# Values' copy in DRAM: rows by place then chunk, window reads that alternate between the two partition halves

## The chip, the core and the metric

The kernel runs on one core of a Trainium2 chip. A core has a matrix engine (TensorE, here PE, with its weight loads as PEld), three engines for elementwise work (VectorE or DVE, ScalarE or ACT, GpSimd or POOL), SyncE (SP), which only issues transfers, and 16 DMA engines that move all data between DRAM (HBM) and the on-chip memory of 128 partitions. Transfers issued by POOL go through queue q0, those of SP through q1, those of ACT through q10; all three share the 16 DMA engines. The metric is the device time of one execution in microseconds.

## The reference

Chunked attention over 4 batches, 8 heads, 768 tokens, head size 64, followed by a mixture of experts that takes the two best of 8 experts per token. Only the windows matter here.

```python
chunk, left_ctx, right_ctx = (32, 16, 8)
for c in range(nc):                       # 24 chunks of 32 tokens
    l_start = max(0, c * chunk - left_ctx)
    r_end = min(S, c * chunk + chunk + right_ctx)
    k_full = np.concatenate([mem_k, k[:, :, l_start:r_end]], axis=2)
    v_full = np.concatenate([mem_v, v[:, :, l_start:r_end]], axis=2)
    a = softmax(scale * q_c @ k_full.T)
    out[:, :, c_start:c_end] = np.matmul(a, v_full)
# then: x = out as [3072, 512]; logits = x @ w_gate, noisy top 2 of 8,
# out = sum of top2_w * (relu(x @ w1[e]) @ w2[e])
```

Each chunk of 32 queries sees 8 memory rows and a window of 56 rows: 16 before the chunk, the chunk itself, 8 after.

## The kernel before

There are two stages, attention with routing and then the experts. Attention runs over 4 batches of 3 steps, each step t covering 256 tokens. A step has these parts. `scores` (L402 on) multiplies queries by keys and subtracts the row maximum on VectorE. `exps` takes the exponential on ScalarE. `turn_p` transposes the probabilities on PE. `values` (L441 on, products at L453) multiplies them by the values, and VectorE scales the result (L460). `turn_x` and `gate` compute the router's logits. Before the first step of a batch `turn` transposes its queries and keys on PE (L393), and VectorE and ScalarE copy them out (L531 for the first batch, L549 for the others). A finished batch is stored to DRAM as `xd` by `keep_x` (L485, issued by ACT, the last part by SP). The routing lists pick rows of `xd` for the experts, whose products are L714 and L726; their weights are loaded by POOL (L78 to L87).

Values need the 64 rows of a window on the partitions: for one chunk, 8 memory rows and then 56 rows of the sequence, for even heads (par 0) on partitions 0 to 63 and for odd heads (par 1) on 64 to 127. This regrouping goes through DRAM. For each batch b:

- `load_v` (L117) loads the values from f32 to bf16 into `vn`: 128 partitions, six tokens each.
- `spread_v` (L368, two POOL copies) reorders the heads into `vp`, so that a token's row has 256 numbers of the even heads and then 256 of the odd ones.
- `window_v` writes `vp` to the DRAM tile `vd` as rows of 1 KB in the order of the sequence (L374, one transfer issued by SP, 128 runs of 6 KB). Then POOL issues two transfers of the memory rows (L378) and four window reads (L383). A read takes place k of every chunk's window to partition k: for each of 32 (or 24) partitions, 24 runs of 512 B that lie 32 KB apart in `vd`. The first span (r0 = 0) covers places 0 to 31 and the second (r0 = 32) places 32 to 55; the order is par 0 first span, par 0 second span, par 1 first span, par 1 second span.

`vd` has two tiles, for even and odd batches; so have the destination `vb`, the keys and the queries. 16 rows before and 16 after the sequence are filled with zeros once (L156); scores of places outside the sequence are set to a large negative number (L418, L420), so that they get no weight.

The order of all POOL's transfers is pinned as written: v0, k0, q0, then memory rows and window reads of batch 0, v1, q1, k1, the spread of batch 1, v2, memory rows and window reads of batch 1, q2, k2, the spread of batch 2, v3, and so on to the weights of experts 0 to 2. POOL works in order: while it waits for the write of `vd` to land, nothing behind is issued. PE, VectorE, ScalarE and SP follow an order written out by hand (L516 to the end of attention): turns of the next batch's queries and keys stand between the steps of this one.

Semaphores of transfers rotate over eight per kind of queue, so a transfer also waits until the one eight before it has landed.

Of the kernel before, what the change touches and what calls it, by code (L numbers as in the profile page):

```python
# [22 lines left out]
def kernel(  # L23
# [14 lines left out]
    nc = tc.nc  # L38
# [65 lines left out]
    def scratch(n):  # L104
        scol[0] -= n
        return wflat[:, scol[0]:scol[0] + n]
    xrow = [scratch(SO * Dm).rearrange("p (s r) -> p s r", s=SO) for _ in range(2)]
    vn = scratch(H * SO * D).rearrange("p (h c) -> p h c", h=H)
# [5 lines left out]
    vd = [tc.dram_tile([S + CH, Dm], BF16, name=f"vd{i}") for i in range(2)]  # L114

    def load_nat(t, x, b):
        pin(nc.gpsimd.dma_start(out=t, in_=x[b].rearrange("h (p s) d -> p h (s d)", s=SO)))  # L117

    def load_v(b):
        load_nat(vn, v, b)  # L120
# [29 lines left out]
    vp = keep.tile([128, H * SO * D], BF16, name="vp")  # L150
# [3 lines left out]
    for i in range(2):  # L154
        for r0, n in ((0, LC), (LC + S, CH - LC)):
            nc.sync.dma_start(out=vd[i][r0:r0 + n, :], in_=zeros[0:n, :])  # L156


# [4 lines left out]
    for b in range(B):  # L163
        nc.sync.dma_start(out=mvs[b * NM:(b + 1) * NM], in_=mem_v[b].rearrange("h m d -> m h d"))
    mvn = keep.tile([B * NM, Dm], BF16, name="mvn")
# [200 lines left out]
    def spread_v(b):  # L366
        for par in range(2):
            pin(nc.gpsimd.tensor_copy(  # L368
                out=vp.rearrange("p (s a c d) -> p a c s d", s=SO, a=2, c=HP)[:, par],
                in_=vn.rearrange("p (c a) (s d) -> p a c s d", a=2, s=SO)[:, par]))  # L370

    def window_v(b):
        t, o = vb[b % 2], vd[b % 2]
        nc.sync.dma_start(out=o[LC:LC + S, :].rearrange("(p s) c -> p (s c)", s=SO), in_=vp)  # L374
        for par in range(2):
            p0 = par * 64
            cols = slice(par * 256, (par + 1) * 256)
            pin(nc.gpsimd.dma_start(out=t[p0:p0 + NM, par], in_=mvn[b * NM:(b + 1) * NM, cols].unsqueeze(1).to_broadcast([NM, NCH, 256])))  # L378
        for par in range(2):
            p0 = par * 64  # L380
            cols = slice(par * 256, (par + 1) * 256)
            for r0, n in ((0, CH), (CH, WIN - CH)):
                pin(nc.gpsimd.dma_start(out=t[p0 + NM + r0:p0 + NM + r0 + n, par],  # L383
                                        in_=o[r0:r0 + S, cols].rearrange("(c k) w -> k c w", k=CH)[0:n]))
# [601 lines left out]
```

## Time and profile before

| | |
|---|---|
| time, median of 3 runs (lowest, highest) | 360.43 us (359.46, 362.16) |
| the profiled execution: its own time, its span | 358.42 us, 356.7 us |
| PE, DVE, ACT, POOL busy | 80%, 48%, 38%, 38% of the span |
| PE busy in 144 to 350 us (three windows) | 204.3 of 206 us |
| PE busy in 22 to 127 us (five windows) | 72.1 of 105 us |
| mean granted PE clock | 0.867 |
| queue q0 | 34240 packets, 46.82 MB, 73.2% of 16 engines' span |
| write of `vd`, issue to landing | 768 KB x4, median 9.0 us |
| window reads, issue to landing | 384 KB x8, median 13.0 us; 288 KB x8, median 13.3 us |
| POOL's time at an issue of a window read | 745 ns |
| POOL's copies of L368 | 8, 1469 ns each |

The profile is of one execution. A share of busy time is a mean over the span, which here has two stages with different limits; so it is read by stage. The DMA share adds the time of all packets over 16 engines. It goes above 100%, since an engine has more than one packet under way. The trace also holds each packet of a DMA engine with its queue, size, start and duration, called the packet records below; they do not name the engine. Times in the text are microseconds from the start of the span.

### The profile page before, as it was taken

The page shows a single profiled execution, that of the slowest core. Times are in us where ns is not written, and L with a number is a line of the kernel's source. Part 1 is how long each engine was busy: PE and PEld are TensorE (multiplying, and loading weights), DVE is VectorE, ACT ScalarE, POOL GpSimd, SP SyncE. Part 2 cuts the span into 40 slices and gives each one's busy share as a digit, 9 for nine tenths or more (in the row PEclk, how much of TensorE's full clock was granted, in tenths as well). Part 3 has the DMA queues.
Part 4 walks back from the last instruction along what each step waited for, and adds up shares of the span by engine and source line. Part 5 has one row for each costly group of instructions (what it writes and reads, how often), then busy time and mean ns, then how long its engine had stood idle before and what let it go on. Part 6 is the DMA issues. An engine that isn't in the chain of part 4 may idle for free.

```text
span 356.7 us, 7042 instructions
## 1 busy us (share of the span) xinstructions
PE 285.9 (80%) x2934; PEld 186.3 (52%) x2955; DVE 170.3 (48%) x349; ACT 136.9 (38%) x189; POOL 134.3 (38%) x181
## 2 busy tenths in 40 slices
PE   0356577777847732999999999999999999999991
PEld 0245455666736621865544465664455775565540
DVE  7656456699689885531133302954310334223221
ACT  8813645564645610144322343213243222243310
POOL 6460573354453036706530744332580122201122
PEclk9995655565687865699999999999999999999998
DMA  8999999999999999499999999961289971100012
GB/s 122 235 171 169 245 174 208 251 198 211 247 156 208 253 249 180 106 194 143 178 196 235 209 173 252 159 119 51 87 166 189 208 184 54 53 2 2 25 47 81
DMA packets 49866, 56.97 MB, mean 160 GB/s; under 512 B 16931, under 2 KB 39523, under 8 KB 49828
## 3 DMA queue, kind: packets, MB, share of 16 engines
q0 software_dynamic: 34240, 46.82, 73.2%
q1 hardware_dynamic: 13920, 6.62, 10.9%
q10 hardware_dynamic: 1668, 3.02, 2.4%
q8 instruction: 25, 0.41, 0.5%
q14 instruction: 13, 0.11, 0.1%
HBM read 70.39 MB, written 13.96 MB: 236 GB/s over the span
## 4 chain that ended last, share of the span: by engine, by line
PE 33%; issue 20%; POOL 5%; DVE 4%; DMA 3%; POOLq 1%; ACT 0%; DVEq 0%
PE p_h L714 18%; PE p_y L726 13%; POOL out_dram L677 4%; DMA out_dram<-y,main_dst 1%; DMA xTt<-xt 1%; DMA xt<-xd,main_src 1%; POOL xt L671 1%; DVE w_all L460 1%; PE p_xt L691 0%; POOL w_all L844 0%; POOLq L981 0%; DVE mx L423 0%; DVE sc L425 0%; ACT xT L472 0%; PE ps_o L453 0%
## 5 line engine op out<-in xcount | busy, mean ns | idle before, releaser
L714 PE MATMUL p_h<-xTt,w_all 128*128 128x256 bf16 (+3 forms) x669 | 102.7, 313 | 0.7 <-DVE xTt L692 0.5
L726 PE MATMUL p_y<-w_all,h 128*128 128x512 bf16 x446 | 102.3, 379 | 0.9
L714 PEld LDWEIGHTS <-w_all 128*128 128x128 bf16 x736 | 70.0, 101 | 36.3 <-issue 0.7
L702 ACT ACTIVATE h<-p_h 128x512 bf16<-128x512 f32 (+1 forms) x81 | 44.7, 551 | 95.9 <-PE p_h L714 88.3
L726 PEld LDWEIGHTS <-h 128*128 128x128 bf16 x464 | 45.3, 98 | 51.6
L700 DVE TENSOR_SCALAR h<-p_h 128x512 bf16<-128x512 f32 (+1 forms) x49 | 31.0, 633 | 82.8 <-PE p_h L714 73.7
L677 POOL DMA_INDIRECT out_dram<-y,main_dst x28 | 30.9, 1103 | 87.9 <-DVE y L732 75.4
L732 DVE SCALAR_TENSOR_TENSOR y<-p_y,main_w,y 128x512 f32<-128x512 f32 x28 | 21.0, 750 | 39.2 <-PE p_y L726 32.5
L393 PE MATMUL p_t<-identb,w_all 128*64 128x128 bf16 x384 | 20.6, 288 | 23.0 <-DMA w_all<-in_k_dram 13.4
L671 POOL DMA_INDIRECT xt<-xd,main_src x28 | 27.9, 997 | 24.2 <-DMA xTt<-xt 13.0
L730 ACT ACTIVATE y<-p_y,main_w 128x512 f32<-128x512 f32 x28 | 19.2, 687 | 37.0 <-PE p_y L726 36.0
L393 PEld LDWEIGHTS <-w_all 128*64 128x64 bf16 x384 | 18.1, 155 | 25.2 <-DMA w_all<-in_k_dram 13.9
L439 ACT COPY pT<-p_p 128x1024 bf16<-128x1024 bf16 x12 | 12.1, 1012 | 27.5 <-PE p_p L436 27.5
L383 POOL DMA_DIRECT2D w_all<-vd x16 | 11.8, 747 | 23.8 <-DMA vd<-vp 19.3
L460 DVE TENSOR_TENSOR w_all<-ps_o,rs 128x512 bf16<-128x512 f32 x24 | 15.6, 686 | 8.2 <-PE ps_o L453 7.8
L415 PE MATMUL ps_s<-kT,qT 128*32 128x112 bf16 x384 | 11.6, 276 | 7.2 <-DVE kT L549 5.4
L368 POOL COPY vp<-w_all 128x1536 bf16<-128x1536 bf16 x8 | 11.5, 1469 | 13.2 <-DMA w_all<-in_v_dram 13.2
L430 ACT ACTIVATE pb<-sc 128x1024 bf16<-128x1024 f32 x12 | 12.8, 1063 | 8.9 <-DVE sc L425 8.7
L549 DVE COPY kT<-p_t 64x768 bf16<-64x768 bf16 x12 | 11.5, 955 | 7.9 <-PE p_t L393 7.8
L425 DVE TENSOR_TENSOR sc<-ps_s,mx 128x1024 f32<-128x1024 f32 x12 | 14.7, 1225 | 0.8
L423 DVE TENSOR_REDUCE mx<-ps_s 128x16 f32<-128x1024 f32 x12 | 14.7, 1224 | 0.8 <-PE ps_s L415 0.5
L453 PE MATMUL ps_o<-w_all,pT 128*32 128x128 bf16 x384 | 10.9, 280 | 3.3 <-issue 2.0
(172 smaller groups left out, 284.0 us busy)
## 6 DMA issues: line engine op xcount, KB each, us to landing
w_all<-in_moe_w_dram POOLq DMA_DIRECT2D x16, 1024.0 KB, 20.7
w_all<-in_moe_w_dram POOLq DMA_DIRECT2D x8, 512.0 KB, 13.8
w_all<-in_v_dram POOLq DMA_DIRECT2D x4, 768.0 KB, 12.1
w_all<-in_k_dram POOLq DMA_DIRECT2D x4, 768.0 KB, 20.9
w_all<-in_q_dram POOLq DMA_DIRECT2D x4, 768.0 KB, 18.1
vd<-vp SPq DMA_DIRECT2D x4, 768.0 KB, 9.0
w_all<-vd POOLq DMA_DIRECT2D x8, 384.0 KB, 13.0
w_all<-vd POOLq DMA_DIRECT2D x8, 288.0 KB, 13.3
```

The source lines that it names most:

```text
L393: nc.tensor.transpose(out=p_t[own(par), s, :], in_=src[:, 2 * pair + par, s * D:(s + 1) * D], identity=identb, tile_position=(0, par * 64))
L423: nc.vector.tensor_reduce(out=mx, in_=s3, axis=AX, op=Alu.max)
L425: nc.vector.tensor_tensor(out=sc, in0=s3, in1=bc(mx, KW), op=Alu.subtract)
L460: nc.vector.tensor_tensor(out=xr[:, j, 0:Dm].rearrange("p (h d) -> p h d", h=H), in0=ps_o[:, j].rearrange("p c a d -> p (c a) d"), in1=bc( ...
L671: i = nc.gpsimd.indirect_dma_start(out=xts[key].bitcast(I32), out_offset=None, in_=xd, in_offset=bass.IndirectOffsetOnAxis(ap=ix, axis=0))
L677: i = nc.gpsimd.indirect_dma_start(out=out, out_offset=bass.IndirectOffsetOnAxis(ap=ix, axis=0), in_=y, in_offset=None, bounds_check=N - 1 ...
L700: nc.vector.tensor_scalar(out=out_, in0=in_, scalar1=0.0, scalar2=None, op0=Alu.max)
L702: nc.scalar.activation(out=out_, in_=in_, func=Act.Relu)
L714: nc.tensor.matmul(out=o, lhsT=w(kp * F + f * 128, 128), rhs=x[:, kp], start=(kp == 0), stop=(kp == KP - 1))
L726: nc.tensor.matmul(out=p, lhsT=h[:, (f * n + j) * 128:(f * n + j + 1) * 128], rhs=w(KP * F + f * Dm, Dm), start=(f == 0), stop=(f == FB - 1))
L730: nc.scalar.activation(out=y, in_=p, func=Act.Copy, scale=weight)
L732: nc.vector.scalar_tensor_tensor(out=y, in0=p, scalar=weight, in1=y, op0=Alu.mult, op1=Alu.add)
```

## The change

Three things change in how values go through DRAM.

The values are loaded on 96 partitions of eight tokens each in place of 128 of six, and the spread works on these 96.

The DRAM tile gets another order. It is [8 groups, 98 rows, 512]: a group holds four places of the window (place k of a chunk, k = 4 g to 4 g + 3), a place has 24 rows, one for each chunk, and two rows of room stand behind the four places. The write becomes eight transfers issued by SP. Each takes every fourth of the 96 partitions and four of its eight tokens: 24 x 4 runs of 1 KB. Rows of chunk c stand at c in one half of the places and at c + 1 in the other, so that a read that begins one row later sees the next chunk. Rows at the seams hold another place's data; they belong to places outside the sequence, whose scores get no weight.

The window reads have the same destinations, 32 or 24 partitions, and in the words of the change use eight engines a transfer, with the halves in turn. Their source is now 8 (or 6) groups of 96 runs of 512 B that lie 1 KB apart. The order becomes first span par 0, first span par 1, second span par 0, second span par 1. The zero fills move behind the loads of the memory rows and write 4 rows each.

By the listing of instructions, SP issues 28 transfers more, POOL as many as before; the order of all other instructions on the five engines is unchanged.

```diff
-    vn = scratch(H * SO * D).rearrange("p (h c) -> p h c", h=H)
+    SV = 8
+    VP = S // SV
+    vn = scratch(H * SV * D).rearrange("p (h c) -> p h c", h=H)
...
-    vd = [tc.dram_tile([S + CH, Dm], BF16, name=f"vd{i}") for i in range(2)]
+    VG = 4 * NCH + 2
+    vd = [tc.dram_tile([CH // 4, VG, Dm], BF16, name=f"vd{i}") for i in range(2)]
...
     def load_v(b):
-        load_nat(vn, v, b)
+        pin(nc.gpsimd.dma_start(out=vn[0:VP], in_=v[b].rearrange("h (p s) d -> p h (s d)", s=SV)))
...
-        for r0, n in ((0, LC), (LC + S, CH - LC)):
-            nc.sync.dma_start(out=vd[i][r0:r0 + n, :], in_=zeros[0:n, :])
+        for g0, x in ((0, 0), (LC // 4, VG - 2)):
+            nc.sync.dma_start(out=vd[i][g0:g0 + LC // 4, x], in_=zeros[0:LC // 4, :])
...
     def spread_v(b):
         for par in range(2):
             pin(nc.gpsimd.tensor_copy(
-                out=vp.rearrange("p (s a c d) -> p a c s d", s=SO, a=2, c=HP)[:, par],
-                in_=vn.rearrange("p (c a) (s d) -> p a c s d", a=2, s=SO)[:, par]))
+                out=vp.rearrange("p (s a c d) -> p a c s d", s=SV, a=2, c=HP)[0:VP, par],
+                in_=vn.rearrange("p (c a) (s d) -> p a c s d", a=2, s=SV)[0:VP, par]))

     def window_v(b):
         t, o = vb[b % 2], vd[b % 2]
-        nc.sync.dma_start(out=o[LC:LC + S, :].rearrange("(p s) c -> p (s c)", s=SO), in_=vp)
+        for x in range(CH // SV):
+            c0, g = divmod(LC // SV + x, CH // SV)
+            for z in range(2):
+                nc.sync.dma_start(out=o[2 * g + z, c0:c0 + 4 * NCH].rearrange("(k c) w -> c k w", c=NCH),
+                                  in_=vp[x:VP:CH // SV, z * 4 * Dm:(z + 1) * 4 * Dm].rearrange("p (k w) -> p k w", w=Dm))
...
-        for par in range(2):
-            p0 = par * 64
-            cols = slice(par * 256, (par + 1) * 256)
-            for r0, n in ((0, CH), (CH, WIN - CH)):
-                pin(nc.gpsimd.dma_start(out=t[p0 + NM + r0:p0 + NM + r0 + n, par],
-                                        in_=o[r0:r0 + S, cols].rearrange("(c k) w -> k c w", k=CH)[0:n]))
+        for x, n in ((0, CH), (1, WIN - CH)):
+            for par in range(2):
+                p0 = par * 64 + NM + x * CH
+                cols = slice(par * 256, (par + 1) * 256)
+                pin(nc.gpsimd.dma_start(out=t[p0:p0 + n, par].rearrange("k c w -> k (c w)"),
+                                        in_=o[0:n // 4, x:x + 4 * NCH, cols]))
```

More of the change, by code (lines that the diff above doesn't have):

```diff
@@ L149 @@
     nc.vector.tensor_copy(identf, identb[0:NG, 0:NG])
-    vp = keep.tile([128, H * SO * D], BF16, name="vp")
+    vp = keep.tile([128, SV * Dm], BF16, name="vp")
     lg_all = keep.tile([128, NG, 2 * E], F32, name="lg_all")
@@ L153 @@
     nc.vector.memset(zeros, 0.0)
-    for i in range(2):
-        for r0, n in ((0, LC), (LC + S, CH - LC)):
-            nc.sync.dma_start(out=vd[i][r0:r0 + n, :], in_=zeros[0:n, :])
     mks = keep.tile([128, 2, D], F32, name="mks")
@@ L164 @@
         nc.sync.dma_start(out=mvs[b * NM:(b + 1) * NM], in_=mem_v[b].rearrange("h m d -> m h d"))
+    for i in range(2):
+        for g0, x in ((0, 0), (LC // 4, VG - 2)):
+            nc.sync.dma_start(out=vd[i][g0:g0 + LC // 4, x], in_=zeros[0:LC // 4, :])
     mvn = keep.tile([B * NM, Dm], BF16, name="mvn")
```

## The prediction

> **What bounds the kernel now.** I read the slices of the span first. TensorE (PE) is full only from slice 17 on, the expert stage; in the first 16 slices, about 140 us of attention, it is half busy and the DMA engines are full.
>
> ```profile
> PE   0356577777847732999999999999999999999991
> DMA  8999999999999999499999999961289971100012
> ```
>
> The chain of waits that ended last runs from 144 us to 257 us almost wholly over PE lines L714 and L726, so the expert stage keeps its length; it starts when attention ends. The change touches only attention, so the question is what attention waits for. The timeline of PE answers that: these are its idle times behind loads after 30 us (the last bracket is the idle time and its releaser).
>
> ```profile
> 32.79 1.04 PE L453 MATMUL ps_o<-w_all,pT 128*32 128x128 bf16 x32 [1.30 <-DMA w_all<-vd]
> 39.77 2.43 PE L393 MATMUL p_t<-identb,w_all 128*64 128x128 bf16 x48 [1.25 <-DMA w_all<-in_q_dram]
> 45.62 2.13 PE L393 MATMUL p_t<-identb,w_all 128*64 128x128 bf16 x36 [3.43 <-DMA w_all<-in_k_dram]
> 61.15 1.04 PE L453 MATMUL ps_o<-w_all,pT 128*32 128x128 bf16 x32 [2.03 <-issue]
> 68.03 1.49 PE L393 MATMUL p_t<-identb,w_all 128*64 128x128 bf16 x24 [2.63 <-DMA w_all<-in_q_dram]
> 98.57 1.46 PE L393 MATMUL p_t<-identb,w_all 128*64 128x128 bf16 x36 [1.44 <-DMA w_all<-in_k_dram]
> ```
>
> With 0.33 us more at 93.98 us these are 12.4 us: the most that faster transfers can give, because between them PE, VectorE and ScalarE hand work to each other. The loads are late because all of POOL's transfers pass one queue (q0) in order: values, keys, queries of a batch and the window reads of L383 between them. The timeline of POOL shows when each batch's four window reads (W0 to W3) are issued, and that POOL idles before them for the write of L374.
>
> ```profile
> 19.97 2.96 POOL L383 DMA_DIRECT2D w_all<-vd  x4 [4.95 <-DMA vd<-vp]
> 35.95 2.88 POOL L368 COPY vp<-w_all 128x1536 bf16<-128x1536 bf16 x2 [10.34 <-DMA w_all<-in_v_dram]
> 45.77 2.96 POOL L383 DMA_DIRECT2D w_all<-vd  x4 [4.42 <-issue]
> 66.19 2.96 POOL L383 DMA_DIRECT2D w_all<-vd  x4 [8.95 <-DMA vd<-vp]
> 90.44 2.96 POOL L383 DMA_DIRECT2D w_all<-vd  x4 [5.43 <-DMA vd<-vp]
> ```
>
> Last, what a window read costs. The first line below is the DMA view of 75 to 80 us, where q0 carries W2 alone; the second that of 126.8 to 128.2 us, where q10 carries plain 4-KB packets (queue: packets, MB, share of 16 engines' time).
>
> ```profile
> q0 software_dynamic: 309, 0.90, 100.7%
> q10 hardware_dynamic: 84, 0.34, 65.7%
> ```
>
> That view puts 92 of the 309 under 2 KB, so 217 packets of 4 KB had 100.7% x 16 x 5 us = 80.6 us, or 78.6 without the small ones: 362 ns each; q10's took 65.7% x 16 x 1.4 / 84 = 175 ns. A window read runs at half speed, 180 GB/s. By the packet records W0 fills 21.4 to 29.9 us, W1 48.6 to 59.6, W2 74.5 to 84.6, W3 95.9 to 107.6.
>
> **Why half.** A window is 1.38 MB, 336 packets. Each of the four reads writes partitions of one half only (8 to 63 or 72 to 127), and par 0 goes before par 1. 362 is about twice 175, in the 32-partition and in the 24-partition reads alike: what I infer is that two engines share one way into that half, while a transfer over 128 partitions has one each. The packets of the first microsecond of W0 (22.2 to 22.9 us) mostly took 159 to 200 ns, before anything backed up, so the source's 512-B runs by themselves aren't slow. The mvn reads of 8 partitions, which are not changed, are worse (253 to 629 ns a packet), which fits.
>
> The Trainium skill (SBUF — State Buffer, Door 1: the DMA port swizzle) has each half of the partitions behind eight ports, and gives 8 ports as 189 GB/s measured; the trace's 180 GB/s agrees. The skill (DMA: Bandwidth & Descriptors, How many engines (k)) takes as many engines as divide the slowest dimension of both sides and, from POOL, moves on round the sixteen: the changed source has 8 groups, and 6 for the second span, so 8 engines a transfer and then 6, the halves beside each other.
>
> **Part by part.**
> Reads: x=0 for both halves, then x=1 for both. The change speaks of eight engines a transfer. If so, the halves run beside each other with one engine to a way, and an engine gets 12 packets of the first span and, on 12 of the 16, 12 of the second: 24 x 175 ns = 4.2 us, with POOL's 0.74-us steps between the four issues 4.9 us. Before: 8.5 to 11.7, say 9.5. Saving 4.6 us a window. Bounds: nothing (halves not side by side), or 11 - 4.2 = 6.8 us. I take 4.6, as it is the row's own factor of two. Issue cost on POOL: 16 at 745 ns as before, the descriptors are as many.
>
> Spread (L368): 2048 instead of 1536 elements a partition on 96 partitions. By 1469 ns for 1536 it is 1.96, so a pair takes 3.9 for 2.9: +1 us before the write of every batch.
>
> Load of values: 1024 packets of 2 KB read in place of 1536 B (written 1 KB for 768 B). By the records 768-B packets ran at 203 GB/s, the 1-KB and 2-KB packets of weights at 205 to 211: nothing.
>
> Write (L374): one transfer of 128 packets of 6 KB at 247 ns becomes eight of 96 packets of 1 KB. The zero fills of L156 are 1-KB packets on the same queue: 46 to 59 ns. SP issues eight at 0.33 us, 2.7 us in all, behind which nothing on SP is due. 24 partitions lie evenly on 12 engines, two each, or on all 16 at best: 64 (48) packets an engine x 59 ns = 3.8 us (2.8), in place of 8 x 247 = 2.0. Alone that is small. But packets of two queues take turns: between 16.5 and 18.5 us the engines took 109 of q1's write packets beside 119 of q0's. With one to 1.25 load packets (79 ns) beside each 1-KB packet and the overlap of 1.3 that the loads show (share 131%), the drain is 64 x (59 + 99) / 1.3 = 7.8 us, where eight large packets took 2.1. Bounds: 2.8 us on a free queue; 64 x (59 + 158) / 1.3 = 10.7 us at two for one. I take 7.8. The bytes on q0 also wait for those engines: 1.3 us more per batch (64 x 59 / 1.3 against 8 x 247 / 1.25).
>
> **The walk.** (v2, k2, q2 are the loads of batch 2.) W0: nothing else is in q0 while it waits (20 to 21.4 us are nearly idle), so the later write counts in full: +1 spread, +1.3 engine time = +2.3. W0 then saves 4.6. Values of batch 1 land 2.3 us earlier (33.7 for 35.95); keys, which share engines with the write, 1 to 2 earlier (45.6 to 44).
> W1: spread to 37.6, first packets 1.5 to 3.5 later as before, 7.8 of drain, 0.9 to land: issued at about 49 where q0 runs dry at about 48. Before, it was issued at 45.77 with 1.5 us of v2 and mvn still ahead: the cover is gone and 1.5 to 3.5 us of q0 are lost. W1 ends near 55.5 (59.6): -4. The 2.03-us wait goes.
> q2 then lands at about 62 (before 68.0): -6 on PE at its turns. k2 comes with batch 2's write and the store of L485 beside it: 55.5 + 4 for q2 + 4 for k2 (a load is 1024 x 79 ns / 16 / 1.3 = 3.9) + 2.9 write + 2.5 store = 69, against a need of 66 (its turns follow q2's by 3 to 4 us): some 2 us given back, -4.
> W2: its write lands at 69 to 72, but q0 has k2, v3 and mvn until 74, so that wait stays covered (before: 66.2 and 74.5). W2 saves 4.6 and leaves q3 and k3 ahead of PE: the waits of 0.33 and 1.44 go too. W3's reads landed at 107.6 and are needed at 114, so its write may slip.
> Sum: -4 - 0.3 - 1.4 = **-6 us** at the end of attention, and the same at the end of the span. Late next are VectorE and ScalarE, whose copies of keys and softmax steps fill the gaps; in the last batch these bind already. Weights follow earlier on q0; POOL's gathers wait for the lists, as before.
> Against the profiled execution (358.4 us, span 356.7) that is 352.4. The median of the runs shown is 360.4, 2.0 above it, so I forecast 354.
>
> **Rivals.**
> A, slower: the halves don't run beside each other, and W reads stay at 9.5 us. Then only the costs remain: W0 +2.3; W1's write starts 3.3 late and lands at 53.4, q0 dry at 52.2, first packet at 54.8: +6.2 for everything behind. Price +6: 366. It decides once the read saving is under about 2 us a window. For it: which engine takes which packet is not in the records, and mvn's two halves, 48 packets on neighbouring transfers, show no gain. Against: the factor of two in both spans.
> The skill (SBUF — State Buffer, Can I just issue two DMAs to hit both halves?) measured +6% for two transfers on the two halves: they serialize. By it a window would save 6% of 9.5, 0.6 us, and the time would be this rival's; its reason, that each sprays over all sixteen engines, would not hold with eight.
> B, no change: the reads are quick but the write takes it. At 10.7 us of drain W1 is issued 3 us later still, k2 later by the same, and the gain falls to 0 to 2: 358 to 361. For it: POOL already waits for the write 19.3 us in three of the four batches.
> C, more: the write drains as on a free queue; no bubble at W1, k2 in time: -10, 350. The 12.4 us bound it.
>
> **How the numbers follow.** Forecast 0.45, C 0.10, B 0.20, A 0.25. A measurement of this kernel tells about 1% (3.6 us) from no change. Forecast and C are faster but for a sliver: 0.53; B with that sliver is same: 0.22; slower 0.25. The range 347 to 365 holds the forecast, C, B and the lower part of A.
>
> **What would show it.** In the profile after: packets of W near 175 to 200 ns and 300 GB/s or more in a window (A: 350 ns); 3072 packets of 1 KB on q1; POOL's wait at the window reads longer than 19.3 us; PE's waits at 61 and 68 us gone and the first expert matmul near 138 us instead of 144. It is wrong if the window reads stay slow, or if the write lands more than 12 us after its spread.

## The result

The changed kernel is slower. Its median is 376.3 us (375.4 to 376.8, four runs) against 360.8 us (359.5 to 362.2, four runs) for the kernel before on the same chip: a ratio of 1.043, with an interval of 1.038 to 1.047. A second comparison, on another chip, gave the same ratio (1.043, 1.039 to 1.047). The forecast of 354 us and its range of 347 to 365 are missed, and the sign is wrong.

The profiled execution took 376.8 us, with a span of 375.2 us (before: 358.4 and 356.7). The slices of the span, as before in fortieths, show first where it went.

```profile
PE   0470664086783674279999999999999999999991
DMA  8949994998986999949899999992069992100012
```

After the first slice, TensorE has two more empty ones in attention, the fourth and the eighth, where it was busy for 60% and 70% before. DMA, which stood at 9 in slices 2 to 16, drops to 4 in the third and again in the seventh: a little ahead of PE's empty slices, the DMA engines have little to do. The expert stage is as long as before: its first product stands at 162.25 us, so it takes 213.0 us of the span, where it took 212.6 from 144.14 us. Of the 18.5 us that this span is longer, 18.1 are lost in attention. The timeline of PE in the changed kernel, with the idle time and its releaser in the bracket, answers to the one in the prediction (L453 and L393 are now L458 and L398):

```profile
38.47 1.04 PE L458 MATMUL ps_o<-w_all,pT 128*32 128x128 bf16 x32 [8.87 <-DMA w_all<-vd]
45.70 2.34 PE L398 MATMUL p_t<-identb,w_all 128*64 128x128 bf16 x48 [1.50 <-DMA w_all<-in_q_dram]
49.54 2.13 PE L398 MATMUL p_t<-identb,w_all 128*64 128x128 bf16 x36 [1.50 <-DMA w_all<-in_k_dram]
75.20 1.05 PE L458 MATMUL ps_o<-w_all,pT 128*32 128x128 bf16 x32 [13.43 <-issue]
86.41 2.13 PE L398 MATMUL p_t<-identb,w_all 128*64 128x128 bf16 x36 [1.85 <-DMA w_all<-in_k_dram]
```

The first products of batches 0 and 1 with their values wait 8.9 and 13.4 us, where they waited 1.3 and 2.0. For the second the profile names no releaser ("issue"), but the last landing of batch 1's window reads stands at 74.8 us, just ahead of it. That product comes 14.05 us later than before (75.20 for 61.15), and that of batch 2, which waits for no load, 14.2 us later. First the kernel before, then the one after:

```profile
88.55 1.04 PE L453 MATMUL ps_o<-w_all,pT 128*32 128x128 bf16 x32
```

```profile
102.73 1.04 PE L458 MATMUL ps_o<-w_all,pT 128*32 128x128 bf16 x32
```

So batches 0 and 1 are the loss, and the rest of the 18.1 us comes in the last batch and after it. The timeline of POOL says what the windows wait for.

```profile
25.63 3.94 POOL L388 DMA_DIRECT2D w_all<-vd  x4 [9.94 <-DMA vd<-vp]
42.40 3.73 POOL L369 COPY vp<-w_all 96x2048 bf16<-96x2048 bf16 x2 [10.23 <-DMA w_all<-in_v_dram]
60.94 3.95 POOL L388 DMA_DIRECT2D w_all<-vd  x4 [12.41 <-DMA vd<-vp]
86.31 3.94 POOL L388 DMA_DIRECT2D w_all<-vd  x4 [13.46 <-DMA vd<-vp]
114.11 3.94 POOL L388 DMA_DIRECT2D w_all<-vd  x4 [13.52 <-DMA vd<-vp]
```

From the end of the spread to the issue of the window reads, the write took 7.5, 6.9, 11.4 and 10.2 us before; now it takes 11.9, 14.8, 15.9 and 18.3 us. In the groups of instructions POOL's idle time behind the write went from 19.3 us in three batches to 49.3 us in all four. First the kernel before, then the one after (busy, mean ns | idle before it, releaser):

```profile
L383 POOL DMA_DIRECT2D w_all<-vd x16 | 11.8, 747 | 23.8 <-DMA vd<-vp 19.3
```

```profile
L388 POOL DMA_DIRECT2D w_all<-vd x16 | 15.8, 993 | 49.3 <-DMA vd<-vp 49.3
```

The same lines show a price that I had not foreseen: the issue of one window read went from 747 to 993 ns. The instructions of the write's own line (shortest, median, longest, in ns) show another, before and after:

```profile
L374 SPq DMA_DIRECT2D vd<-vp x4: 319/334/355, 12.5 to 80.2; - x4
```

```profile
L378 SPq DMA_DIRECT2D vd<-vp x32: 744/753/3909, 13.8 to 109.2; - x32
```

One issue of the new form occupies SP for 753 ns, and in batches 0 and 1 one of the eight stood for 3.8 and 3.9 us. From the first issue to the end of the eighth it took 9.5, 9.65, 6.35 and 14.1 us. In the last batch the time went between two issues: semaphores rotate over eight, the eighth write has that of a store of `xd` issued by ACT at 101.4 us, and SP waited until that store had landed (us in total, times, longest):

```profile
SPq L378 <- DMA xd<-w_all: 7.8, 1, 7.8
```

That wait is off the path, as no product of the last batch waits for a load. The packet records divide the time of the write, from the first issue to the issue of the window reads (us):

| batch | issue to first packet, before / after | first packet to end of the last | end of the last to the window reads' issue |
|---|---|---|---|
| 0 | 3.5 / 2.4 | 2.7 / 8.3 | 1.2 / 1.1 |
| 1 | 1.5 / 1.4 | 4.6 / 12.0 | 0.9 / 1.4 |
| 2 | 4.6 / 4.1 | 5.5 / 9.6 | 1.3 / 2.1 |
| 3 | 4.5 / 4.1 | 4.8 / 13.0 | 1.0 / 1.3 |

Only the middle part grew by much. In batches 0 and 3 the last packet ended 1.2 and 2.9 us after the last issue, so there the issues set the pace; in batches 1 and 2 it ended 3.8 and 7.4 us after it, beside loads. While the write of batch 2 runs beside loads, between 75 and 83 us, the DMA view of the changed kernel has

```profile
q0 software_dynamic: 1387, 1.12, 88.1%
q1 hardware_dynamic: 812, 0.74, 35.1%
```

that is 0.74 of 0.79 MB of the write in 8 us, close to the 7.8 of the prediction. In this batch the queue q0 stays full through the wait (92.6% of the engines from 75 to 86 us), and batch 2 falls no further behind. In batch 1 it runs empty: from 57 to 63 us the DMA view has no line of q0 at all, only

```profile
q10 hardware_dynamic: 120, 0.74, 30.5%
q1 hardware_dynamic: 170, 0.15, 8.0%
```

and in batch 0 it shows 0.1% for q0 from 21.5 to 27 us.

The reads did get quicker, by less than a third of what I had said. By the packet records, from the first packet to the landing of the last, with the mean of the 4-KB packets:

| window | before | after | kernel before, order of reads changed (below) |
|---|---|---|---|
| W0 | 10.3 us, 366 ns | 10.0 us, 286 ns | 8.7 us, 333 ns |
| W1 | 11.3 us, 426 ns | 10.3 us, 299 ns | 9.6 us, 372 ns |
| W2 | 11.4 us, 399 ns | 10.0 us, 300 ns | 9.3 us, 348 ns |
| W3 | 11.9 us, 434 ns | 9.4 us, 292 ns | 10.4 us, 369 ns |

The best stretch of the changed kernel, 64.7 to 67.5 us in W1, moves 275 GB/s; before, W2 moved 180, and by the packet records the best 2.8 us of any window about 203:

```profile
DMA packets 391, 0.77 MB, mean 275 GB/s; under 512 B 204, under 2 KB 206, under 8 KB 390
```

### The profile page after: what moved, and what is told of

Same layout as the page of the kernel before. It is cut to its first block, busy times and chain, and to the rows that moved or that the text cites. A ratio compares the mean times of both kernels' runs of the same rounds, so it can differ in the third digit from the quotient of the medians.

```text
span 375.2 us, 7086 instructions
## 1 busy us (share of the span) xinstructions
PE 284.3 (76%) x2934; PEld 184.5 (49%) x2955; DVE 173.1 (46%) x349; ACT 137.0 (37%) x189; POOL 141.3 (38%) x181
## 4 chain that ended last, share of the span: by engine, by line
PE 32%; issue 19%; POOL 5%; DMA 3%; DVE 3%; ACT 1%; POOLq 1%; ACTq 0%
PE p_h L719 17%; PE p_y L731 13%; POOL out_dram L682 3%; DMA out_dram<-y,main_dst 1%; DMA xt<-xd,main_src 1%; DMA xTt<-xt 1%; POOL xt L676 1%; DVE w_all L465 1%; PE ps_o L458 1%; ACT pT L444 0%; PE p_xt L696 0%; POOL w_all L849 0%; PE p_list L353 0%; POOLq L986 0%; ACT xT L477 0%
## 5 line engine op out<-in xcount | busy, mean ns | idle before, releaser
L398 PE MATMUL p_t<-identb,w_all 128*64 128x128 bf16 x384 | 21.0, 286 | 17.7 <-DMA w_all<-in_k_dram 11.9
L388 POOL DMA_DIRECT2D w_all<-vd x16 | 15.8, 993 | 49.3 <-DMA vd<-vp 49.3
L398 PEld LDWEIGHTS <-w_all 128*64 128x64 bf16 x384 | 17.9, 153 | 20.3 <-DMA w_all<-in_k_dram 12.5
L458 PE MATMUL ps_o<-w_all,pT 128*32 128x128 bf16 x384 | 10.3, 270 | 22.9 <-issue 14.1
L369 POOL COPY vp<-w_all 96x2048 bf16<-96x2048 bf16 x8 | 15.0, 1917 | 13.5 <-DMA w_all<-in_v_dram 13.5
L458 PEld LDWEIGHTS <-pT 128*32 128x32 bf16 x384 | 7.8, 120 | 23.3 <-issue 23.1
L420 PE MATMUL ps_s<-kT,qT 128*32 128x112 bf16 x384 | 11.2, 275 | 5.8 <-DVE kT L554 5.4
L554 DVE COPY kT<-p_t 64x768 bf16<-64x768 bf16 x12 | 11.4, 954 | 8.0 <-PE p_t L398 7.8
## 6 DMA issues: line engine op xcount, KB each, us to landing
w_all<-in_v_dram POOLq DMA_DIRECT2D x4, 768.0 KB, 11.2
w_all<-vd POOLq DMA_DIRECT2D x8, 288.0 KB, 10.2
```

Source lines behind the costliest of these rows:

```text
L388: pin(nc.gpsimd.dma_start(out=t[p0:p0 + n, par].rearrange("k c w -> k (c w)"), in_=o[0:n // 4, x:x + 4 * NCH, cols]))
L398: nc.tensor.transpose(out=p_t[own(par), s, :], in_=src[:, 2 * pair + par, s * D:(s + 1) * D], identity=identb, tile_position=(0, par * 64))
L458: nc.tensor.matmul(out=ps_o[r * CH:(r + 1) * CH, j, pair], lhsT=pT[:, j * HP + pair, r * CH:(r + 1) * CH], rhs=vb[b % 2][:, :, (tp * 2 + j ...
```

## The experiments

The kernel before differs by 1% from chip to chip (medians from 358.9 to 362.8 us). So ratios to the kernel before on the same chip are compared, and 1% is 3.6 us. Theory and rival at the start: the loss is the write's, of which the reads' gain covers a part (theory); or the reads are no better and the loss is theirs too (rival A of the prediction).

### What each part of the write costs alone

Three kernels put one part of the change into the kernel before. `runs_1k` makes the packets small and nothing else:

```diff
-    vd = [tc.dram_tile([S + CH, Dm], BF16, ...
+    vd = [tc.dram_tile([S + CH, Dm + 8], BF16, ...
-        nc.sync.dma_start(out=o[LC:LC + S, :].rearrange("(p s) c -> p (s c)", s=SO), in_=vp)
+        nc.sync.dma_start(out=o[LC:LC + S, 0:Dm].rearrange("(p s) c -> p s c", s=SO), in_=vp.rearrange("p (s c) -> p s c", s=SO))
```

> The kernel before with one change: a row of the DRAM copy is 8 numbers longer, so that its one write goes out as 768 runs of 1 KB in place of 128 of 6 KB, on 16 engines; one issue, reads as before. Theory 'small packets' (the write loses because its 1-KB packets take turns with q0's): 48 packets an engine x (59 + 79) / 1.3 = 5.1 us for 2.1, so landings 3 to 6 us later, 366 to 370 us. Rival 'eight issues' (the write loses because SP issues eight transfers at 0.75 us): 361 us, as before.

`eight_6k` cuts the one write into eight transfers and leaves its runs at 6 KB:

```diff
-        nc.sync.dma_start(out=o[LC:LC + S, :].rearrange("(p s) c -> p (s c)", s=SO), in_=vp)
+        for z in range(8):
+            nc.sync.dma_start(out=o[LC + z * 96:LC + z * 96 + 96, :].rearrange("(p s) c -> p (s c)", s=SO),
+                              in_=vp[z * 16:z * 16 + 16])
```

> The kernel before with its write cut into eight transfers of 16 partitions, runs of 6 KB as before. 'Small packets': 361 to 362 us, the packets are the same. 'Eight issues': the last transfer is issued 2.3 us later (0.33 us each, the row of before) to 5.3 us later (0.75 each, the row of after), so 364 to 368 us.

`load_96` takes only the load and the spread on 96 partitions, with one write of 96 runs of 8 KB:

```diff
-        load_nat(vn, v, b)
+        pin(nc.gpsimd.dma_start(out=vn[0:VP], in_=v[b].rearrange("h (p s) d -> p h (s d)", s=SV)))
...
-        nc.sync.dma_start(out=o[LC:LC + S, :].rearrange("(p s) c -> p (s c)", s=SO), in_=vp)
+        nc.sync.dma_start(out=o[LC:LC + S, :].rearrange("(p s) c -> p (s c)", s=SV), in_=vp[0:VP])
```

> The kernel before with only the load and the spread changed to 96 partitions of eight tokens; one write of 96 runs of 8 KB, reads as before. Every theory: the spread takes 0.9 us more before each write, 361 to 364 us.

Measured: `runs_1k` 364.4 us, ratio 1.012 (1.004 to 1.019); `eight_6k` 366.05 us, 1.015 (1.008 to 1.022); `load_96` 366.5 us, 1.013 (1.006 to 1.019). Each part costs about 4 to 5 us by itself; their sum is 3.9%. `runs_1k` came out between its two forecasts, `load_96` above its one. None of the three is the loss alone. Small packets make the write land later without an issue more; and eight issues do so with large packets. The line of `eight_6k` shows that the long stalls of SP come with large packets too, so small runs are not their reason (beside them SP waited twice, 14.5 us in all, for stores of `xd`):

```profile
L375 SPq DMA_DIRECT2D vd<-vp x32: 302/419/4368, 13.1 to 100.0; - x32
```

That `load_96` costs anything was against the prediction, which had put the load at nothing and the spread at +1 us. `spread_long` separates the longer copy: two thirds of the second copy are done twice.

```diff
+        pin(nc.gpsimd.tensor_copy(
+            out=vp.rearrange("p (s a c d) -> p a c s d", s=SO, a=2, c=HP)[:, 1, :, 0:4],
+            in_=vn.rearrange("p (c a) (s d) -> p a c s d", a=2, s=SO)[:, 1, :, 0:4]))
```

> The kernel before with two thirds of the second copy of the spread done twice: about 1 us more of POOL ahead of each write, the same bytes, everything else untouched. It parts the two halves of load_96 (+4.3 us). If that loss was the longer spread alone: 365 to 366.5. If it was the load on 96 partitions or the write in 96 runs of 8 KB: the spread costs its 1 us at batch 0 and little more, 362.5 to 364 beside a kernel before of 361 to 362.

Measured: 360.95 us, ratio 0.999 (0.995 to 1.004). One more microsecond of POOL ahead of each write (1.04 us by its timeline) costs nothing that shows; the interval reaches up to 1.4 us, so a microsecond that counts once can't be excluded. The longer spread is then at most a part of the loss of `load_96` (4.5 us, 2.2 at the low end of its interval). Its trace shows where time goes: W1 and W3, both read from the second `vd` tile, take 14.5 and 13.9 us (11.3 and 11.9 before). The two stretches below hold little else than window reads. First `load_96` from 53 to 57 us, then the kernel before from 50 to 54 us:

```profile
DMA packets 151, 0.43 MB, mean 108 GB/s; under 512 B 49, under 2 KB 49, under 8 KB 150
```

```profile
DMA packets 216, 0.65 MB, mean 162 GB/s; under 512 B 58, under 2 KB 58, under 8 KB 216
```

The reads are the same instructions, from a tile of the same shape. Why they run at two thirds of the rate stays open.

`four_writes` asks whether the number of issues carries the loss of the changed kernel. Its places have 25 rows, so that one transfer writes eight places.

```diff
-    vd = [tc.dram_tile([CH // 4, VG, Dm], BF16, ...
+    vd = [tc.dram_tile([CH, NCH + 1, Dm], BF16, ...
-            for z in range(2):
-                nc.sync.dma_start(out=o[2 * g + z, c0:c0 + 4 * NCH]...
+            nc.sync.dma_start(out=o[8 * g:8 * g + 8, c0:c0 + NCH].rearrange("k c w -> c k w"),
+                              in_=vp[x:VP:CH // SV].rearrange("p (k w) -> p k w", w=Dm))
```

> The changed kernel with places of 25 rows and the write in four transfers of 192 runs of 1 KB; reads on 8 (6) engines of 25 rows a place, 4% more bytes. 'Small packets': as many packets in the same turns, 374 to 377 us. 'Eight issues': half the issues, landing some 3 us earlier a window, 369 to 372 us, if an issue costs 0.75 us whatever it carries.

Measured: 375.5 us, ratio 1.038 (1.031 to 1.045), within the interval of the changed kernel. POOL's waits for the write are 9.2, 10.5, 11.1 and 11.4 us, for 9.9, 12.4, 13.5 and 13.5 with eight issues. Half the issues save 0.7 to 2.3 us of this wait and no time that this comparison can tell.

### Is it the wait?

`after_free` and `before_free` take the wait away without a race: the window reads come from a DRAM tile of zeros that is filled once, so they don't wait for the write, which is still done. Both leave the values of the sequence out of the result.

```diff
-                                        in_=o[0:n // 4, x:x + 4 * NCH, cols]))
+                                        in_=vz[0:n // 4, x:x + 4 * NCH, cols]))
```

> The changed kernel with the same thing left out: window reads take a tile of zeros, eight writes run and nobody waits for them. Theory 'wait' (the reads did get faster, and the whole loss is the wait for a later write): below before_free by 3 to 8 us, 350 to 356 us. Rival 'reads' (the new reads give nothing, or cost by their longer issue on POOL): as before_free or slower, 357 to 365 us.

> The kernel before, but its window reads take a DRAM tile of zeros that is filled once at the start; the write still runs, nobody waits for it. Left out: the values of the sequence (the result holds the memory rows alone). It shows what the wait for the write costs before: by PE's idle times 1.3 to 4 us, less some 2 us for the fill at the start: 357 to 361 us under every theory.

Measured: 363.25 us for the changed kernel without the wait, ratio 1.006 (1.002 to 1.011); 369.9 us for the kernel before without it, 1.026 (1.016 to 1.036). The first says that 13 of the 15.5 us go with the wait, although it is above the 350 to 356 that the theory had; POOL's spreads of batches 2 and 3 still wait there for the write, 7.9 and 2.7 us, because they fill the same `vp`. The second is far outside its forecast of 357 to 361. The pair can't be read as the gain of the reads: in `before_free` the filling of the zeros held the first window read back until 21.3 us, in `after_free` until 16.7, and in both the reads run beside the writes. So two kernels keep every byte and move only places on POOL.

`after_cover` fills the wait: the values of batch 1 are issued ahead of W0, queries and keys of batches 2 and 3 ahead of W1 and W2.

```diff
         window_v(0)
+        load_v(1)
+        read_v(0)
...
                 window_v(b + 1)
                 if b + 2 < B:
                     load_kq(b + 2)
+                read_v(b + 1)
+                if b + 2 < B:
                     spread_v(b + 2)
```

(`window_v` here ends with the memory rows; `read_v` issues the four window reads.)

> The changed kernel with the values of batch 1 and the queries and keys of batches 2 and 3 issued by POOL between a batch's write and its window reads; all transfers are the same, only these places on POOL change. Theory 'exposed wait' (the loss is that all of q0 stands still while POOL waits for the eight writes, 12 to 18 us a batch): 4 us of values fit into the first wait and 8 us of queries and keys into the second and third, so the turns at 49.5 and 79.5 to 83.4 us come 4 and 10 us earlier; the loads run beside the write and make it land 2 to 4 us later, which holds the window reads back by that. Net 6 to 10 us better than the changed kernel's 376: 366 to 370. Rival 'engine time' (the small packets and the slower reads take the time themselves, whatever stands beside them): at most 2 us better, 374 to 377. Rival 'reads late': the window reads of batches 1 and 2 now bound the first product of values (75.2 and 102.7 us); then 372 to 376 with longer idle times of PE ahead of these products.

Measured: 373.0 us, ratio 1.034 (1.027 to 1.041): 3.2 us better than the changed kernel by the ratios, half of what the theory had, and within the range of the rival 'reads late'. The lines of POOL and PE say why. POOL in `after_cover`:

```profile
32.81 3.76 POOL L369 COPY vp<-w_all 96x2048 bf16<-96x2048 bf16 x2
50.11 2.96 POOL L391 DMA_DIRECT2D w_all<-vd  x3 [9.34 <-DMA vd<-vp]
```

PE in `after_cover`:

```profile
75.47 1.04 PE L461 MATMUL ps_o<-w_all,pT 128*32 128x128 bf16 x32 [12.13 <-DMA w_all<-vd]
```

The spread of batch 1 starts 9.6 us earlier than in the changed kernel and W1 is issued 10.8 us earlier, and yet the product comes at 75.5 us as before: now 8 us of queries and keys stand in the queue ahead of W1. `after_v1` keeps the first move and drops the second.

> The changed kernel with one transfer moved: the values of batch 1 are issued by POOL ahead of the window reads of batch 0, where POOL waits 10 us for the write. With queries and keys moved as well, batch 1's spread began at 32.8 us for 42.4, and yet its first product stayed at 75.5 us, because its window reads then stood behind 8 us of queries and keys. Theory 'chain' (values load, spread, write, reads, product follow one another; what the write takes is added to that chain, whatever fills the queue): without those 8 us in front, batch 1's reads are issued at about 50 us and end at about 61, its first product comes at 63 to 65 instead of 75.2, and the end of attention comes 6 to 10 us earlier: 366 to 370. Rival 'throughput' (the queue's work to be done is what counts, in whatever order): the first product stays at 72 us or later, and the time at 373 to 376.

POOL in `after_v1`:

```profile
32.84 3.77 POOL L369 COPY vp<-w_all 96x2048 bf16<-96x2048 bf16 x2
50.50 3.95 POOL L391 DMA_DIRECT2D w_all<-vd  x4 [11.49 <-DMA vd<-vp]
```

PE in `after_v1`:

```profile
65.98 1.05 PE L461 MATMUL ps_o<-w_all,pT 128*32 128x128 bf16 x32 [2.75 <-issue]
```

Measured: 371.75 us, ratio 1.026 (1.022 to 1.030). The wait of 13.4 us is down to 2.75, the product comes at 65.98 us (63 to 65 expected, 72 or later by the rival), and the gain is 1.7%, 6 us by the ratios; in absolute time it is just short of the 366 to 370 that were expected, beside a kernel before that took 362.5 on that chip. In batches 0 and 1 the chain is load, spread, write, reads, product, one after the other. What the write takes longer is added to that chain, and starting the chain earlier wins it back. Filling the queue gained less where the reads stood behind the filling.

### Which part of the reads' change works

`turn_order` is the kernel before with the order of its four reads changed and nothing else: 32 and 24 partitions on sixteen and twelve engines as before, first span of both halves, then second span of both halves.

```diff
-        for par in range(2):
-            ...
-            for r0, n in ((0, CH), (CH, WIN - CH)):
+        for r0, n in ((0, CH), (CH, WIN - CH)):
+            for par in range(2):
```

> The kernel before with only the order of its four window reads changed to first span par 0, par 1, second span par 0, par 1, on 16 (12) engines. If the order by itself puts the halves beside each other: 354 to 358 us. If each engine works its transfers off in order and so all 16 are in one half at a time: 360 to 362 us.

Measured: 358.9 us, ratio 0.992 (0.987 to 0.996): 3 us faster than the kernel before, between the two forecasts. Its windows are in the table above, 1.5 to 2.1 us shorter each. `after_order` is the counterpart: the changed kernel with the order put back, eight and six engines a transfer as there.

> The changed kernel with the order of the four window reads put back (both spans of par 0, then both of par 1), still eight and six engines a transfer, writes untouched. If the halves side by side are what sped up the reads: the first span's packets go from 159 to 215 ns back to some 300 to 360 ns, a window takes 2 to 4 us longer, and the time rises by 1 to 4 us over the changed kernel's 376: 377 to 380. If the reads are quicker there only because the queue has run empty ahead of them: packets and time stay, 375 to 377.

Measured: 382.2 us, ratio 1.055 (1.051 to 1.060), 1.2% or 4.5 us slower than the changed kernel. The first product of batch 1 moves from 75.20 to 78.53 us:

```profile
78.53 1.04 PE L458 MATMUL ps_o<-w_all,pT 128*32 128x128 bf16 x32 [16.10 <-issue]
```

By the packet records its windows take 11.7, 15.3, 11.2 and 10.6 us, for 10.0, 10.3, 10.0 and 9.4 in the changed kernel; its time is above the 377 to 380 that were expected. So the halves in turn do help, in both kernels. Whether the eight engines do (no record names the engine of a packet, so the numbers of engines are the change's own words for the two forms) is told by two kernels with the changed kernel's eight writes, but places of 25 rows, which let a read take 32 or 24 partitions as in the kernel before. `reads_16` reads in the order of the kernel before, `reads_16_turn` in the changed order.

```diff
-                pin(nc.gpsimd.dma_start(out=t[p0:p0 + n, par].rearrange("k c w -> k (c w)"),
-                                        in_=o[0:n // 4, x:x + 4 * NCH, cols]))
+                pin(nc.gpsimd.dma_start(out=t[p0:p0 + n, par], in_=o[0:n, x:x + NCH, cols]))
```

> The changed kernel with every place of the DRAM copy 25 rows long, the same eight writes of 96 runs of 1 KB, but window reads as before: 16 (12) engines a transfer, par 0 before par 1. Theory 'wait' with faster reads: the reads go back from some 7.3 to 9.5 us a window, and about two of the four windows are exposed, so slower than the changed kernel by 3 to 8 us, 379 to 384 us. Rival 'reads' (the new reads give nothing): 376 us or less.

> The changed kernel's eight writes with window reads of 32 and 24 partitions on sixteen and twelve engines (as reads_16, 377.5), and with the changed order, both halves of the first span and then both of the second. In the changed kernel the order alone was worth 5.9 us (376.3 for 382.2), in the kernel before 3 us (358.9 for 362.2). If the order is the whole gain of the reads and eight engines a transfer are not needed for it: 371 to 375, below the changed kernel's 376.3. If the halves run beside each other only with eight engines each: 376 to 378, as reads_16.

Measured: `reads_16` 377.5 us, ratio 1.039 (1.032 to 1.047); `reads_16_turn` 373.5 us, ratio 1.040 (1.034 to 1.046). In microseconds the second is 4 better, by the ratio it is not better at all: the kernel before took 362.2 us on the one chip and 358.9 on the other. Nothing follows from the pair, so both were measured again beside the changed kernel on one chip.

> The changed kernel, beside the two below on one chip, since the runs of the kernel before differ by 1% from call to call (358.9 to 362.5) and a difference of 3 us between calls is no difference. Expected 4.3% over the kernel before, as at first.

> As reads_16: sixteen and twelve engines, halves one after the other. If eight engines with the halves in turn are what speeds the reads: 1% above the changed kernel or more. If they bring nothing over sixteen engines: within 0.5% of it (its first ratio was 1.0393 for the changed kernel's 1.0427).

> As reads_16_turn: sixteen and twelve engines, halves in turn. If the order brings on these writes what it brought on the kernel before (0.85%): 3 us below reads_16 on the same chip. If its first ratio is right (1.0398 for 1.0393): no difference from it.

Measured, beside 362.8 us: the changed kernel 378.6 us, 1.043 (1.039 to 1.047); `reads_16` 378.3 us, 1.044 (1.040 to 1.047); `reads_16_turn` 375.7 us, 1.034 (1.030 to 1.038). Here the order is worth 0.9% with sixteen engines, as in the kernel before (0.85%); the first pair had shown none of it. Eight engines with the order changed equal sixteen engines with the old order, and are 0.9% behind sixteen engines with the order changed. A possible reason shows in the lines of POOL: an issue of the eight-engine form takes 993 ns, of the other about 740, which is 1 us a window.

### A version that beats both

`turn_v1` is `turn_order` with the values of batch 1 issued ahead of W0, as in `after_v1`; `turn_cover` also moves queries and keys ahead of W1 and W2.

> The kernel before with the changed order of the four window reads (as turn_order, 358.9) and with the values of batch 1 issued ahead of the window reads of batch 0, where POOL waits 7.5 us for the write and the queue is empty for 1.4 us. If the empty queue counts: keys of batch 1 land 2 us earlier, and their waits on PE (1.25 and 3.43 us before) shrink: 357. If batch 0's window reads are what PE needs first (1.3 us of wait at 32.8 us before), they come 2 us later beside the load, and nothing is gained: 359 to 361.

> turn_v1 and also queries and keys of batches 2 and 3 ahead of the window reads of batches 1 and 2, as in after_cover but on the kernel before with its one write. If the wait for the write costs the kernel before as well: 354 to 356. If not, since the queue there has other loads during that wait, the window reads of batch 1 end some 6 us later (63 for 57) against a product at 59 us, and of batch 2 at 88 against 79: 2 to 5 us slower than turn_v1, 360 to 363.

Measured, beside 360.4 us: `turn_v1` 355.35 us, ratio 0.987 (0.979 to 0.994); `turn_cover` 362.6 us, 1.008 (1.005 to 1.012). The first has the shortest time of this study, though its interval overlaps that of `turn_order`. W0 does come later, and the product with it (35.45 us for 31.59 in `turn_order`), as was feared; but the keys of batch 1, which PE waited for in the kernel before and in `turn_order`, now come in time. These are PE's waits for loads between 38 and 50 us in `turn_order`, of which `turn_v1` has none:

```profile
38.38 2.77 PE L393 MATMUL p_t<-identb,w_all 128*64 128x128 bf16 x48 [0.83 <-DMA w_all<-in_q_dram]
44.23 2.13 PE L393 MATMUL p_t<-identb,w_all 128*64 128x128 bf16 x36 [3.08 <-DMA w_all<-in_k_dram]
```

Yet attention doesn't end earlier for it. In the profiles the first product of every batch comes later in `turn_v1`, by 3.9, 0.8, 1.2 and 3.7 us, and the first expert product stands at 141.04 us for 139.10. Its shorter span (351.6 us for 354.3) comes from the expert stage, 210.6 us for 215.2, which neither change touches and which takes 210.6 to 215.7 us in the profiles of this study. So it is not shown that the moved values add anything to the order of the reads.

`turn_cover` confirms what `after_cover` showed: loads put ahead of W1 hold its product back, to 68.6 us for 59.9 in `turn_v1`.

## Why the prediction was wrong

**What bounds the kernel, and where the end comes from:** right. The expert stage kept its length (213.0 us for 212.6), and nearly all that was lost was lost in attention, behind the window reads of batches 0 and 1.

**Write (L374), the step that failed.** "SP issues eight at 0.33 us, 2.7 us in all" took the duration of one form of transfer for another: the new form takes 753 ns, and with stalls the eight took 6.35 to 14.1 us. The packets then came as slowly as they were issued, or beside loads. For W1 the prediction had "first packets 1.5 to 3.5 later as before, 7.8 of drain, 0.9 to land"; measured are 1.4, 12.0 and 1.4. For W0 it had only "+1.3 engine time" for the write; measured are 4.4 us. The bound of 10.7 us for the drain fell as well, in two of four batches. From its spread the write took 11.9 to 18.3 us. The text had its own alarm, a landing more than 12 us after the spread; three of the four batches passed it.

**The walk.** W0 was to be issued 2.3 us later and was issued 5.7 us later (25.63 for 19.97): 1.3 of it lie ahead of the write (the spread starts 0.4 later and takes 0.85 longer) and 4.4 are the write. W0's reads, which were to give back 4.6, gave back 0.3 by the table. So the values of batch 1, queued behind them, were 6.5 us later instead of 2.3 us earlier. The write of batch 1 added 7.9 us, W1 was issued at 60.94 us and not at 49, and the product came 14.05 us late. Of q0 "1.5 to 3.5 us" were to be lost there; it was empty for some 6. For W2 the walk was right that "q0 has k2, v3 and mvn until 74, so that wait stays covered", if 12 us later: POOL waited 13.5 us, q0 stayed full, and batch 2 has no more lag than batch 1.

**Reads: half right.** "The halves beside each other" do run faster: the order alone gains 0.85 to 1.2% in three pairs of kernels, and nothing in a fourth. That eight engines with a way each would bring a packet to 175 ns is not borne out, and whether two engines shared one way before was not tested. The factor of two was taken from a ratio of two packet durations, 362 and 175 ns. Measured are 286 to 300 ns, and a window that took 10.3 to 11.9 us takes 9.4 to 10.3: 1.3 us less on average instead of 4.6. The start value was low too: the prediction's own windows of before, 8.5 to 11.7 us, have a mean of 10.3 and not 9.5, and up to the landing of the last packet it is 11.2. The price of eight engines was missing: "16 at 745 ns as before, the descriptors are as many" became 993 ns, and `after_order` against `reads_16_again` shows that without the order eight engines are 1.2% slower than sixteen (1.055 to 1.044). In `turn_order`, where the order is all that changes, the four windows together went from 44.9 to 38.0 us, 15% less, and far less than the 50% that I had worked with. The Trainium skill (SBUF — State Buffer, Can I just issue two DMAs to hit both halves?), quoted under rival A, says of two transfers on the two halves that they measured "only +6% over a single one"; the trace of `turn_order`, with its 15%, shows more than the page. Between a row of my own inference and a measured rule that spoke against it, a value in between would have been the better choice.

**Load of values, "nothing":** doubtful. `load_96`, with load, spread and write on 96 partitions, costs 1.3% alone (4.5 us), and `spread_long` shows that the +1 us of the spread, the only price that I had put there, is at most 1.4 us of it. Which of load and write costs the rest, and how they slow later reads, is open.

**Rivals.** Rival A had the right sign, and the wrong reason: its 366 us rested on reads that stay slow and on a write 3.3 us late. B came nearest to the mechanism ("the reads are quick but the write takes it"), but priced the write by a slower drain alone and let it only cancel the gain. That the write could cost more than all that the reads can bring was in no case, since each case took SP's 0.33 us from the trace of before.

**Not fully explained:** the sum. By the ratios the three parts alone make 3.9%, and the changed kernel without the gain of the order (`after_order`) is at 5.5%. By the start of the expert stage in the one profile of each, the parts are 6.3 (`runs_1k`), 8.6 (`eight_6k`) and 6.2 us (`load_96`) late, 21.1 together, and `after_order` is 22.1; two profiles of the changed kernel itself differ by 1.5 us there. So the parts may well add up, but the ratios don't show it.

In the last batch the lag grows from 14.5 us at its first product to 17.3 at its second, and loads have no part in it. Between the two, VectorE's running sum for the lists took 0.96 us for 0.19. It ended at 128.65 us, with an operation of POOL that ran beside it (128.61); in the kernel before, POOL was done 2 us ahead of that sum. First the kernel before, then VectorE and POOL after:

```profile
112.54 0.19 DVE L328 TENSOR_TENSOR cum<-cum,red 128x28 bf16<-128x28 bf16 x1
```

```profile
127.69 0.96 DVE L329 TENSOR_TENSOR cum<-cum,red 128x28 bf16<-128x28 bf16 x1
126.17 2.44 POOL L343 TENSOR_TENSOR vals<-ohp,facts 128x1344 bf16<-128x1344 bf16 x1
```

On VectorE, for whose scaling factors PE waits there, the lag goes from 15.15 us at the start of the sum to 15.9 behind it; that VectorE was held up by POOL is not shown beyond these lines. The rest, to 17.3, comes on PE, which ran some of its steps there more slowly (the product for the lists took 1.28 us for 0.74).

## What to carry to other kernels

Before a write is cut into more and smaller transfers to suit the reads, price the whole path until the reader may start, issue by issue, by a form that the trace shows, and ask what waits in order behind that landing; here 1.3 us of quicker reads a window were bought with 4 to 8 us of later landing. When a change has several parts, try the cheapest part alone: the order of four reads, two exchanged lines, held all of the gain that showed. Start a chain of load, regroup, write and read earlier, worth 1.7% in the changed kernel, rather than fill the wait in its middle with loads that then stand ahead of the reads.

## What was unexpected in the hardware

- The time that a transfer's issue holds its queue depends on its form. On SP: 334 ns for 128 runs of 6 KB, 514 ns for 768 runs of 1 KB, a median of 419 ns for sixteen partitions with runs of 6 KB, 753 ns for 24 x 4 (or 24 x 8) runs of 1 KB. On POOL: 745 ns for 32 x 24 runs of 512 B, 993 ns for 8 x 96 of the same runs.
- Of eight issues in a row some held SP for 3.8 to 4.4 us, with runs of 1 KB and of 6 KB alike, and of four issues one for 3.5. What they waited for, no record names. Other waits of SP have a name: eight writes use all eight semaphores, so that one of them met the semaphore of a slow store of `xd` (7.8 us in the changed kernel, 14.5 in two waits in `eight_6k`).
- Two halves of the partitions filled by neighbouring transfers on sixteen engines each, in turn, took 15% less time than one after the other (38.0 us for 44.9 over four windows); eight engines a transfer added nothing to the kernel's time (1.043 for 1.034).
- The same window reads, with little else on the DMA engines for 4 us, ran at 108 GB/s in one kernel and at 162 in another. Two windows of the same kernel that use the same tile were both slow there.
- One microsecond more of POOL's time ahead of each write cost nothing that shows (0.999, 0.995 to 1.004), although the spread stands on the chain of every batch.
